# Loads, rounding and global rows of V for pairs 8 to 15, placed by tables at later quanta

## The chip, the cores and the metric

The kernel runs on one core of one Trainium2 chip. The metric is the device time of one execution in microseconds, as the median of several runs. The engines are named as in the profile: PE is TensorE's matrix multiplies, PEld its weight loads, DVE is VectorE, ACT is ScalarE, POOL is GpSimd and SP is SyncE, which here only issues DMA transfers. Each engine works through its own instructions strictly in the order in which they were recorded, and waits at the first one whose inputs or buffers are not ready.

## The reference: what is computed

An attention with a local band and a few global positions, followed by a two-layer block with a squared ReLU:

```
scores = (q @ k^T) / 8                       # 8 batches x 8 heads, 576 positions, 64 per head
mask   = |i - j| <= 32, or i or j is one of 8 global positions
attn   = softmax(where(mask, scores, -1e9))
x      = (attn @ v), heads side by side      # 4608 tokens x 512
out    = (s * relu(x @ w_in)**2 + b) @ w_out # 512 -> 2048 -> 512
```

Inputs and output are float32 in DRAM; the kernel multiplies in bfloat16.

## The kernel before

**Pairs.** Two heads make a pair: 32 pairs p, counted from 0 as in the code (the words "nine to sixteen" mean p = 8 to 15). Four pairs make a batch bi = p // 4. The 576 keys of a pair lie in 5 chunks of 120, in partitions 8 to 127 of a tile of 128 partitions (V), or 0 to 119 (K, Q); the 8 rows that are left hold the global keys.

**What a pair needs.** K and Q of a pair are loaded as float32 into staging (`natk`, `natq`, four slots each), rounded to bfloat16 on ACT (`round_k` L236 into `natb`, `round_q` L278), and transposed: K from pair 8 on by a DMA transpose on SP (`turn_k` L295, profile line L297), Q up to pair 17 by PE. DVE then writes the eight global columns into the transposed tile (`put_kq` L548, profile line L554), and only then PE may multiply with it. V is loaded into `natv` (`load_v`, L306, profile line L226; staging slot (p - 2) % 4), rounded into a ring `vring` of five slots (`cast_v` L309, profile line L312; ring slot p % 5), and its eight global rows are copied into the ring by a small DMA from `gvall` (`put_v` L541, profile line L543). For p of 16 and more, POOL's DMA loads V with the cast on the way, and nothing is rounded by an engine.

**Quanta.** The second half of the work (`moe_quanta` L741) is cut into quanta of four matmuls of 128x512. `run_pair` (L858) walks through eight steps s = 0 to 7 of a pair and issues one quantum in most of them, so that a place in the program is a pair (p, s): pair p, step s. Attention's work is hung on such places. `VISITS` (L47) says where PE visits a pair: at (8, 7), (9, 7), (10, 6), (11, 5) and then (12, 3), (13, 3) and so on. A visit to p multiplies Q and K of the second part of pair p and the first part of pair p + 1 (`visit` L849, tiles `pss` and `psw`), and then multiplies the probabilities of an earlier step with V (`put_out`, tile `po`): pairs 8 and 9 are first needed from `vring` at (9, 7), pairs 10 and 11 at (11, 5), pairs 12 and 13 at (13, 3), pairs 14 and 15 at (15, 3).

**What sets the order.** Everything is recorded by hand: `at(s, f, ...)` in the loop over p (L1120 to L1211) puts an operation behind the quanta of step s, `run_pair` puts others ahead of them. K and Q of later pairs, the K transposes, the V loads up to pair 15 and the global rows of pairs 8 to 15 all go out on SP, in one sequence. POOL rounds V of pairs 8 to 12, scatters global columns into the second block's input (L733), gathers and loads the pieces of w_out for the bias (`wpiece` L1099, profile line L1101). ACT rounds V of pairs 13 to 15.

**Where V of pairs 8 to 15 stands before.** Loads: pair 8 ahead of the steps of p = 4, pair 9 ahead of p = 5, pair 10 at (6, 5), 11 and 12 at (7, 5), 13 at (8, 5), 14 at (9, 5), 15 at (10, 5) (L1150 to L1154). Rounding: 8 and 9 at (7, 2), 10 at (8, 2), 11 at (9, 2), 12 at (10, 2) on POOL, 13 at (11, 2), 14 at (11, 4), 15 at (12, 4) on ACT (L888 to L900). Global rows: 8 and 9 at (7, 7), then pair p + 2 at (p, 7) (L1188 to L1191).

Of the kernel before, what the change touches and what calls it, by code (L numbers as in the profile page):

```python
# [34 lines left out]
NPAIR = B * H // 2  # L35
# [9 lines left out]
VCAST = 16  # L45
SOFT = 16
VISITS = {8 * p + {8: 7, 9: 7, 10: 6, 11: 5}.get(p, 3): p for p in range(JOIN, NPAIR)}  # L47
KT0 = 16
NX = 3
N6 = NCH * KC // NJ  # L50
# [25 lines left out]
def view(ap, *dims):  # L76

    return bass.AP(
        tensor=ap.tensor, offset=ap.offset, ap=[list(ap.ap[0])] + [list(d) for d in dims]
    )  # L80
# [3 lines left out]
def kernel(  # L84
# [12 lines left out]
    nc = tc.nc  # L97
# [33 lines left out]
    def bank(name):  # L131
# [4 lines left out]
        elif name in ("psh", "psg"):  # L136
            ago = min((when[0] - x for x in VISITS if x <= when[0]), default=8)
            left = min((x - when[0] for x in VISITS if x > when[0]), default=8)
            near = ago < 2 or left < 3 or ago == 4
# [64 lines left out]
    def v_slot(p):  # L204
        return p - 2 if p in (4, 5) else (p if p < 4 else p - 2) % NV
# [89 lines left out]
    def turn_k(p):  # L295
        kts[p] = kqp.tile([P, KT0 + NCH * P], BF16, tag="kt", name="kt")
        nc.sync.dma_start_transpose(  # L297
            out=kts[p][:, KT0:].rearrange("p (c x) -> p c x", x=P), in_=natb[:, p % NV]
        )
# [6 lines left out]
    def load_v(eng, p):  # L306
        load_nat(eng if p < VCAST else nc.gpsimd, "v", p)

    def cast_v(eng, p):  # L309
        if p >= VCAST:  # L310
            return
        eng(out=vring[:, p % NVR], in_=(natk if p in (4, 5) else natv)[:, v_slot(p)])  # L312
# [235 lines left out]
    def put_kq(p, which=(0, 1)):  # L548
        bb, x = divmod(p, 8)
        if p >= NSIX:  # L550
            ktile[p] = kts[p][:, KT0 - NG : KT0 - NG + LQ]
        for i in which:
            dst, src_ = ((ktile[p], gkt[bb]), (qbufs[p % 3][:, HB:], gqt[bb % 2]))[i]
            V(  # L554
                out=view(dst, [P, NCH], [1, NG]),
                in_=view(src_[:, NG * x : NG * x + NG], [0, NCH], [1, NG]),
            )
# [31 lines left out]
    def trans_a(p, later=later):  # L589
        ps = trans("k", p)  # L590
        kt = ktp.tile([P, LQ], BF16, tag="kt", name="kt")
        ktile[p] = kt[:]

        def evac():
            (A if p == 5 else V)(
                out=view(kt[:, NG:], [P, NCH], [NJ, KC // NJ], [1, NJ]),
                in_=view(ps, [KC // NJ, NCH], [1, KC // NJ], [NP6, NJ]),
            )
            if 3 < p < 6:
                put_kq(p)  # L600

        later.append(evac)
# [233 lines left out]
    def step():  # L836
        if pending:
            pending.pop(0)()

    def open_batch(bi):  # L840
        gsums[bi] = nrm.tile([P, 2, 2, 3, NG], FP32, tag="gs", name="gs")
# [5 lines left out]
    A, V, G = nc.scalar.copy, nc.vector.tensor_copy, nc.gpsimd.tensor_copy  # L847
# [10 lines left out]
    def run_pair(p, nq, extra):  # L858

        bi, hp = divmod(p, 4)  # L860
        if hp == 0 and p > 4:
            open_batch(bi)
        for s in range(8) if p > 4 else range(NCH, 8):
            prev, later[:] = list(later), []
            now = []
            at = 8 * p + s
            if p >= JOIN:
                when[0] = at
            if at in VISITS:
                visit(p)  # L870
            elif 4 < p < JOIN and s in ((0, 4) if p % 2 else (1, 3)) or (p, s) == (JOIN, 1):
                qk(p, int(s > 1))
            j = VISITS.get(at + 3, NPAIR) + 1
            if j < QTURN:
                trans_b(j, now)
            for x in (1, 2):
                if VISITS.get(at - x, 0) > JOIN:
                    step()
                    if x == 2 and VISITS[at - x] % 4 == 0:
                        later.append(lambda: scatter(bi - 1))  # L880
            if s < NCH:
                if s in (2, 3) and p <= JOIN:
                    step()
                if (p, s) == (JOIN, 4):
                    later.append(lambda: scatter(bi - 1))
                if s == 1 and p in (6, 7):
                    cast_v(A, p)
                if s == 2 and p == 7:  # L888
                    cast_v(G, 8)
                    cast_v(G, 9)  # L890
                if s == 2 and 7 < p < 11:
                    cast_v(G, p + 2)
                if p > 10:

                    eng, j = {
                        (3, 2): (A, p + 2), (3, 4): (A, p + 3), (0, 4): (A, p + 3),
                        (1, 2): (G, p + 3),
                    }.get((hp, s), (A, NPAIR))
                    if j < NPAIR:
                        cast_v(eng, j)  # L900
            elif s == 5:
                if 4 < p < JOIN - 1:
                    trans_b(p + 1, now)
            if (p, s) == (JOIN - 1, 6):
                trans_b(p + 1, now)
            if s == 4 and 4 < p < NSIX - 1:
                trans_a(p + 1, now)
            if s in (5, 6) and p < JOIN:
                step()
            for f in now + prev:  # L910
                f()
            if VISITS.get(at, 0) > JOIN or 4 < p <= JOIN and s == (4 if p % 2 else 1):
                put_out(p // 2 if p % 2 else p // 2 - 1, 1 - p % 2)
            if s == 3 and p in (6, 7):
                put_v(V, p)
            if s == 7 and p == 4:
                put_v(V, 4)
            if s == 2 and p == 5:
                cast_v(A, 5)
            if s == 3 and p == 5:  # L920
                put_v(V, 5)
            for f in extra.get(s, ()):
                f()
            Q(nq[s])
# [195 lines left out]
    for p in range(4, NPAIR):  # L1120
        bi, hp = divmod(p, 4)
        ex = {}

        def at(s, f, *a, ex=ex):
            ex.setdefault(s, []).append(lambda: f(*a))
# [10 lines left out]
        for s in range(8):  # L1136
            j = VISITS.get(8 * p + s + 2, NPAIR) + 1
# [4 lines left out]
        for j in range(p + 1, min(p + 7, NPAIR)):  # L1142
            x = {
                10: (6, 1), 11: (7, 4), 12: (7, 5), 17: (12, 0), 18: (13, 0), 19: (14, 0),
                20: (14, 4),
            }.get(j, (j - 5 if j < 17 else j - 6, 0))
            if j > 8 and x[0] == p:
                at(x[1], load_nat, nc.sync, "k", j) if x[1] else load_nat(nc.sync, "k", j)
                at(x[1], load_q, j) if x[1] else load_q(j)
        for j in {4: (8,), 5: (9,), 6: (10,), 7: (11, 12)}.get(p, (p + 5,)):  # L1150
            if p < 6:
                load_v(nc.sync, j)
            elif j < VCAST:
                at(5, load_v, nc.sync, j)  # L1154
        if p + 2 >= VCAST and p + 2 < NPAIR:
            at(1, load_v, nc.gpsimd, p + 2)
        if p == 5:
# [7 lines left out]
        for s in range(8):  # L1165
            for j in range(p + 1, min(p + 5, NPAIR)):
# [18 lines left out]
                    at(s, turn_k, j)  # L1185
                if j >= QTURN and (j - 3, 7) == (p, s):
                    at(s, turn_q, j)
        if p == 7:  # L1188
            at(7, put_v, None, 8)
        if p >= 7 and p + 2 < NPAIR:  # L1190
            at(7, put_v, None, p + 2)  # L1191
        if p == 6 or (p % 8 == 4 and 8 < p < NPAIR - 4):
            steps = globals_of((p + 5) // 8)
# [61 lines left out]
```

## Time and profile before

| | |
|---|---|
| median of 3 runs | 340.72 us (338.2, 340.72, 341.35) |
| the profiled execution | 338.03 us, its span 336.4 us |
| PE busy | 317.6 us, 94% of the span |
| PEld / DVE / ACT / POOL busy | 168.6 / 205.1 / 200.0 / 113.2 us |
| moved by DMA | 50.08 MB, of which SP's queue 28.33 MB and POOL's 20.77 MB |

The span is the time from the first to the last event on the core; the profiled execution's own time is 1.6 us more. A busy PE is not a PE at its peak, but idle time of PE is lost for good in a kernel whose PE is busy 94% of the time, unless what follows had to wait anyway. The other engines have slack on average; what counts of them is the one place at which PE waits for them.

### The profile page before, as it was taken

The numbers are of one execution on the slowest core, as the hardware profiler recorded it, in microseconds if no ns is written. First come the engines' busy times: TensorE is split into PE (matmuls) and PEld (weight loads), VectorE is DVE, ScalarE is ACT, GpSimd is POOL, SyncE is SP. The second block draws the span as 40 slices with busy tenths as digits, with TensorE's granted clock in tenths as the row PEclk, the third lists the DMA queues.
The fourth block names the chain that finished last, engine by engine and source line by source line (L and its number), as shares of the span: only waits on it lengthen the run. The fifth ranks groups of instructions, "written<-read, shape, count | busy, mean of one in ns | idle before, by whom it ended". The sixth has DMA issues, their size and how long they took to land.

```text
span 336.4 us, 8685 instructions
## 1 busy us (share of the span) xinstructions
PE 317.6 (94%) x3324; PEld 168.6 (50%) x3364; DVE 205.1 (61%) x540; ACT 200.0 (59%) x337; POOL 113.2 (34%) x220
## 2 busy tenths in 40 slices
PE   7688889799899999999999999999999999999995
PEld 4465344445454555467644444444467544444444
DVE  5479777566669588676765676567556524423422
ACT  3465778657895688557855885687268406404700
POOL 7841751225001405282368316822660030000000
PEclk9999999999999999999999999999999999999999
DMA  8999999997999999999999979993850010011011
GB/s 152 195 208 199 211 196 188 200 213 165 192 174 174 222 210 224 218 154 169 168 220 238 201 131 230 248 98 84 173 116 2 28 68 31 2 63 62 3 52 72
DMA packets 133533, 50.08 MB, mean 149 GB/s; under 512 B 122124, under 2 KB 128588, under 8 KB 133484
## 3 DMA queue, kind: packets, MB, share of 16 engines
q1 hardware_dynamic: 101346, 28.33, 51.3%
q0 software_dynamic: 31792, 20.77, 34.9%
q8 instruction: 26, 0.43, 0.6%
q10 hardware_dynamic: 354, 0.43, 0.4%
q14 instruction: 15, 0.12, 0.1%
HBM read 42.35 MB, written 9.44 MB: 154 GB/s over the span
## 4 chain that ended last, share of the span: by engine, by line
PE 70%; DMA 10%; issue 7%; POOL 5%; DVE 4%; ACT 3%; POOLq 1%; ACTq 0%; DVEq 0%
PE pso L789 31%; PE psh L756 30%; PE po L661 5%; DMA natq<-in_q_dram 4%; DMA kt<-natb 4%; DMA wst<-in_moe_w_out_dram 2%; PE pss L637 2%; ACT r L777 1%; PE psw L637 1%; DVE wsum L1105 1%; POOL xt L733 1%; POOL sixq L199 1%; POOL sixk L199 1%; POOLq L997 1%; DVE g L780 1%
## 5 line engine op out<-in xcount | busy, mean ns | idle before, releaser
L756 PE MATMUL psh<-xt,win_t 128*128 128x512 bf16 (+4 forms) x688 | 129.7, 340 | 2.4 <-POOL xt L733 0.9
L789 PE MATMUL pso<-wout_t,g 128*128 128x512 bf16 (+1 forms) x573 | 126.4, 373 | 2.4 <-issue 2.1
L777 ACT ACTIVATE r<-psh 128x512 bf16<-128x512 f32 x144 | 85.7, 599 | 58.2 <-PE psh L756 56.5
L756 PEld LDWEIGHTS <-win_t 128*128 128x128 bf16 x704 | 63.5, 98 | 58.7 <-issue 2.2
L789 PEld LDWEIGHTS <-g 128*128 128x128 bf16 x592 | 56.2, 98 | 62.9
L780 DVE TENSOR_TENSOR g<-r 128x512 bf16<-128x512 bf16 x144 | 60.3, 422 | 41.1 <-ACT r L777 40.2
L644 ACT ACTIVATE em<-pss 128x840 bf16<-128x840 f32 (+1 forms) x38 | 33.6, 884 | 43.5 <-PE pss L637 43.5
L645 DVE TENSOR_TENSOR em<-em,mask 128x904 bf16<-128x904 bf16 x64 | 38.6, 610 | 33.5 <-ACT em L644 31.2
L733 POOL COPY xt<-xg 128x4 bf16 (+1 forms) x72 | 17.4, 242 | 57.9 <-DVE xt L708 54.0
L809 DVE SCALAR_TENSOR_TENSOR osb<-pso,sb,bias_row 128x512 f32<-128x512 f32 (+1 forms) x25 | 18.2, 727 | 28.7 <-PE pso L789 28.4
L226 POOL DMA_DIRECT2D vring<-in_v_dram x33 | 29.4, 896 | 9.1 <-PE po L661 8.3
L708 DVE TENSOR_TENSOR xt<-po,rep 128x480 bf16<-128x480 f32 (+2 forms) x60 | 24.5, 449 | 3.5 <-ACT rep L718 2.6
L637 PEld LDWEIGHTS <-kt 64*128 64x128 bf16 x384 | 11.9, 99 | 20.2 <-issue 13.2
L644 ACT ACTIVATE em<-psw 128x904 bf16<-128x904 f32 x23 | 21.2, 924 | 0.1
L813 POOL DMA_DIRECT2D out_dram<-osb x16 | 9.1, 566 | 30.3 <-DVE osb L809 25.0
L661 PE MATMUL po<-em,vring 128*32 128x160 bf16 (+3 forms) x840 | 17.9, 220 | 0.7 <-DVE vring L543 0.5
L237 ACT CAST natb<-natk 128x640 bf16<-128x640 f32 x24 | 17.4, 727 | 1.8 <-DMA natk<-in_k_dram 1.8
L637 PE MATMUL pss<-qt,kt 64*128 64x192 bf16 (+4 forms) x228 | 14.6, 240 | 3.0 <-DVE qt L554 2.1
L715 ACT ACTIVATE ln<-po 128x324 f32<-128x324 f32 (+1 forms) x30 | 12.9, 429 | 5.7 <-PE po L661 5.7
L718 ACT ACTIVATE rep<-ln 128x324 f32<-128x324 f32 (+1 forms) x32 | 14.8, 461 | 0.3
L661 PEld LDWEIGHTS <-vring 128*32 128x32 bf16 x896 | 13.7, 98 | 1.1 <-issue 1.0
L661 PE MATMUL po<-em,onesb 128*32 128x192 bf16 (+2 forms) x360 | 11.5, 235 | 0.3 <-ACT rep L718 0.2
(126 smaller groups left out, 242.8 us busy)
## 6 DMA issues: line engine op xcount, KB each, us to landing
natk<-in_k_dram SPq DMA_DIRECT2D x47, 150.0 KB
natv<-in_v_dram SPq DMA_DIRECT2D x28, 150.0 KB
natq<-in_q_dram SPq DMA_DIRECT2D x55, 75.0 KB
wst<-in_moe_w_out_dram POOLq DMA_DIRECT2D x8, 512.0 KB, 6.5
out_dram<-osb POOLq DMA_DIRECT2D x16, 256.0 KB, 3.1
vring<-in_v_dram POOLq DMA_DIRECT2D x31, 75.0 KB, 5.3
out_dram<-osbh POOLq DMA_DIRECT2D x9, 256.0 KB, 3.8
win_t<-in_moe_w_in_dram POOLq DMA_DIRECT2D x4, 512.0 KB
```

What stands on the lines that cost most here:

```text
L226: eng.dma_start(out=dst[r : r + rows, n, c : c + nch, hh], in_=bass.AP(tensor=src[t].tensor, offset=o + c * KC * D, ap=[[D, rows], [KC * D ...
L637: nc.tensor.matmul(ps[:, hh, at : at + hi - lo], ktile[p][r, P * c : P * c + P], qbufs[p % 3][r, lo:hi], start=at == 0, stop=at + hi - lo ...
L644: nc.scalar.activation(em[:], ps[:, :, 0:n], AF.Exp, scale=SCALE)
L645: later.append(lambda: nc.vector.tensor_mul(em[:], em[:], masks[g]))
L661: nc.tensor.matmul(po[DH * j : DH * j + DH, a : a + n], view(vring[:, p % NVR, c, hh, part - 1 :], [2, DH]) if part else onesb[:], emt[(p, ...
L708: nc.vector.tensor_tensor(out=view(xt[:, 2 * g, x0 + t0 :], [NXT, 2], [w, runs], [1, w]), in0=view(po[:, STEP[blk] + col :], [STEP[blk], 2 ...
L733: nc.gpsimd.tensor_copy(out=xt[:, h, S * (bi % NX) : S * (bi % NX) + S][:, :, ds(greg_p[i], 1)], in_=xgs[bi][:, h, i : i + 1],)
L756: nc.tensor.matmul(psh[:, d0 : d0 + n], win_t[:, a, f * P : f * P + P], xt[:, a, x0 : x0 + n], start=(a == 0 and j == 0), stop=(a == 3), s ...
L777: nc.scalar.activation(r[:], psh, AF.Relu)
L780: later.append(lambda g=g, r=r: nc.vector.tensor_mul(g[:], r[:], r[:]))
L789: nc.tensor.matmul(pso[:, 0:nn], gl[f][:, u * P : u * P + P], wout_t[:, f, n0 : n0 + nn], start=(f == 0), stop=(f == 15),)
L809: nc.vector.scalar_tensor_tensor(out=osb[:, 0:nn], in0=pso[:, 0:nn], scalar=s_bc, in1=bias_row[:, n0 : n0 + nn], op0=OP.mult, op1=OP.add,)
```

## The change

Three tables take the place of the conditions that placed V of pairs 8 to 15. `VLOAD` gives the place of each load, `VROUND` the place and engine of each rounding (0 is ACT, 1 is POOL), `VGLOBAL` the place of each copy of global rows.

```
+VLOAD = {
+    8: (6, 6), 9: (7, 2), 10: (7, 6), 11: (8, 2), 12: (8, 6), 13: (9, 4), 14: (10, 4), 15: (11, 4),
+}
+VROUND = {
+    (7, 7): (1, 8), (8, 2): (1, 9), (8, 6): (1, 10), (9, 4): (1, 11), (10, 4): (1, 12),
+    (11, 2): (0, 13), (11, 4): (0, 14), (12, 4): (0, 15),
+}
+VGLOBAL = {
+    8: (8, 3), 9: (8, 4), 10: (8, 7), 11: (9, 6), 12: (10, 6), 13: (11, 7), 14: (12, 7), 15: (13, 7),
+}
...
-                if s == 2 and p == 7:
-                    cast_v(G, 8)
-                    cast_v(G, 9)
-                if s == 2 and 7 < p < 11:
-                    cast_v(G, p + 2)
...
+            if (p, s) in VROUND:
+                eng, j = VROUND[(p, s)]
+                cast_v((A, G)[eng], j)
...
-        for j in {4: (8,), 5: (9,), 6: (10,), 7: (11, 12)}.get(p, (p + 5,)):
-            if p < 6:
-                load_v(nc.sync, j)
-            elif j < VCAST:
-                at(5, load_v, nc.sync, j)
+        for j, x in VLOAD.items():
+            if x[0] == p:
+                at(x[1], load_v, nc.sync, j)
+        for j, x in VGLOBAL.items():
+            if x[0] == p:
+                at(x[1], put_v, None, j)
...
-        if p == 7:
-            at(7, put_v, None, 8)
-        if p >= 7 and p + 2 < NPAIR:
+        if VCAST <= p + 2 < NPAIR:
             at(7, put_v, None, p + 2)
```

No instruction is added or removed. The sequences of PE, DVE and ACT stay as they are, row for row. On POOL one of three roundings ahead of a scatter (that of pair 10) comes behind it. On SP the sequence changes in the stretch from Q of pair 9 to the transpose of K of pair 14. The order of SP's instructions shows it at three places. A row is a line of the kernel, the operation, what is written and read, its shape, and how many follow each other (two loads are one pair's K, V or Q).

First place, SP, before: behind Q of pair 9 come V of 8 and 9, K and Q of 10, V of 10, then the transposes of K 8 and K 9, then K of 11.

```order
L266 DMA natq<-in_q_dram 96x2x384
L226 DMA natv<-in_v_dram 120x5x64 x4
L226 DMA natk<-in_k_dram 120x5x64 x2
L266 DMA natq<-in_q_dram 96x2x384
L226 DMA natv<-in_v_dram 120x5x64 x2
L297 DMA_TRANSPOSE kt<-natb 128x5x128 x2
L226 DMA natk<-in_k_dram 120x5x64 x2
```

First place, SP, with the change (its lines are ten further down):

```order
L276 DMA natq<-in_q_dram 96x2x384
L236 DMA natk<-in_k_dram 120x5x64 x2
L276 DMA natq<-in_q_dram 96x2x384
L307 DMA_TRANSPOSE kt<-natb 128x5x128
L236 DMA natv<-in_v_dram 120x5x64 x4
L307 DMA_TRANSPOSE kt<-natb 128x5x128
L236 DMA natk<-in_k_dram 120x5x64 x2
```

Six V loads (pairs 8, 9 and 10) that stood ahead of the transpose of K 8 now stand behind it; those of pair 10 go still further down.

Second place, SP, before: V of 11 and 12, the transpose of K 10, the global rows of 8 and 9, K and Q of 13, V of 13, the transpose of K 11.

```order
L226 DMA natv<-in_v_dram 120x5x64 x4
L297 DMA_TRANSPOSE kt<-natb 128x5x128
L543 DMA vring<-gvall 8x5x128 x2
L226 DMA natk<-in_k_dram 120x5x64 x2
L226 DMA natq<-in_q_dram 120x5x64 x2
L226 DMA natv<-in_v_dram 120x5x64 x2
L297 DMA_TRANSPOSE kt<-natb 128x5x128
```

Second place, SP, with the change: V of 10, the transpose of K 10, K and Q of 13, V of 11, the global rows of 8 and 9, V of 12, the global rows of 10, the transpose of K 11.

```order
L236 DMA natv<-in_v_dram 120x5x64 x2
L307 DMA_TRANSPOSE kt<-natb 128x5x128
L236 DMA natk<-in_k_dram 120x5x64 x2
L236 DMA natq<-in_q_dram 120x5x64 x2
L236 DMA natv<-in_v_dram 120x5x64 x2
L553 DMA vring<-gvall 8x5x128 x2
L236 DMA natv<-in_v_dram 120x5x64 x2
L553 DMA vring<-gvall 8x5x128
L307 DMA_TRANSPOSE kt<-natb 128x5x128
```

The two copies of global rows no longer follow the transpose at once; six loads stand between.

Third place, SP, before: the transpose of K 11, the global rows of 10, K, Q and V of 14, the transpose of K 12, the global rows of 11, K, Q and V of 15, the transpose of K 13.

```order
L297 DMA_TRANSPOSE kt<-natb 128x5x128
L543 DMA vring<-gvall 8x5x128
L226 DMA natk<-in_k_dram 120x5x64 x2
L226 DMA natq<-in_q_dram 120x5x64 x2
L226 DMA natv<-in_v_dram 120x5x64 x2
L297 DMA_TRANSPOSE kt<-natb 128x5x128
L543 DMA vring<-gvall 8x5x128
L226 DMA natk<-in_k_dram 120x5x64 x2
L226 DMA natq<-in_q_dram 120x5x64 x2
L226 DMA natv<-in_v_dram 120x5x64 x2
L297 DMA_TRANSPOSE kt<-natb 128x5x128
```

Third place, SP, with the change: the transpose of K 11, K and Q of 14, V of 13, the global rows of 11, the transpose of K 12, K and Q of 15, V of 14, the global rows of 12, the transpose of K 13.

```order
L307 DMA_TRANSPOSE kt<-natb 128x5x128
L236 DMA natk<-in_k_dram 120x5x64 x2
L236 DMA natq<-in_q_dram 120x5x64 x2
L236 DMA natv<-in_v_dram 120x5x64 x2
L553 DMA vring<-gvall 8x5x128
L307 DMA_TRANSPOSE kt<-natb 128x5x128
L236 DMA natk<-in_k_dram 120x5x64 x2
L236 DMA natq<-in_q_dram 120x5x64 x2
L236 DMA natv<-in_v_dram 120x5x64 x2
L553 DMA vring<-gvall 8x5x128
L307 DMA_TRANSPOSE kt<-natb 128x5x128
```

V of pair 14, which stood ahead of the transpose of K 12, now stands where V of pair 15 stood, ahead of the transpose of K 13. The place at which ACT rounds pair 14 in its own sequence has not moved.

## Rows read from the trace of the kernel before

**Rows 1.** The page: busy time of the engines, and DMA's busy share in 40 slices.

```profile
PE 317.6 (94%) x3324; PEld 168.6 (50%) x3364; DVE 205.1 (61%) x540; ACT 200.0 (59%) x337; POOL 113.2 (34%) x220
DMA  8999999997999999999999979993850010011011
```

**Rows 2.** Windows: stretch, length, busy time of each engine, clock, DMA share, GB/s.

```profile
40.00:60.00 20.00, 18.78 (x230) 8.90 (x232) 14.83 (x39) 16.20 (x29) 7.58 (x12) 1.00 1.19 194
60.00:80.00 20.00, 17.91 (x182) 8.99 (x176) 11.76 (x30) 10.65 (x18) 8.35 (x16) 1.00 0.93 186
80.00:100.00 20.00, 18.70 (x233) 9.58 (x235) 13.00 (x34) 18.54 (x34) 1.13 (x2) 1.00 1.25 197
100.00:120.00 20.00, 19.68 (x215) 9.96 (x219) 14.94 (x43) 12.85 (x23) 4.88 (x12) 1.00 1.20 193
```

**Rows 3.** Timeline of PE: start, length, instructions, and [idle before, ended by].

```profile
66.50 0.37 PE L637 MATMUL pss<-qt,kt 64*128 64x160 bf16 x6 [1.82 <-DVE qt L554]
...
81.47 0.58 PE L661 MATMUL po<-em,vring 128*32 128x160 bf16 x28
...
89.79 0.37 PE L637 MATMUL psw<-qt,kt 64*128 64x160 bf16 x6 [1.04 <-DVE kt L554]
...
103.26 0.36 PE L637 MATMUL psw<-qt,kt 64*128 64x160 bf16 x6
```

**Rows 4.** Chain of work that ended last: start, length, the transfer waited for.

```profile
61.72 4.24 DMA kt<-natb
...
81.27 8.27 DMA kt<-natb
```

**Rows 5.** Timeline of SP: start and length of issuing, transfers.

```profile
53.29 5.61 SPq L226 DMA_DIRECT2D natv<-in_v_dram  x4
...
60.68 0.94 SPq L226 DMA_DIRECT2D natv<-in_v_dram  x2
61.72 3.35 SPq L297 DMA_TRANSPOSE kt<-natb  x2
...
73.62 1.21 SPq L297 DMA_TRANSPOSE kt<-natb  x1
75.20 1.62 SPq L543 DMA_DIRECT2D vring<-gvall  x2
76.87 1.29 SPq L226 DMA_DIRECT2D natk<-in_k_dram  x2
...
95.43 1.43 SPq L226 DMA_DIRECT2D natv<-in_v_dram  x2
97.03 1.62 SPq L297 DMA_TRANSPOSE kt<-natb  x1
```

**Rows 6.** Timeline of ACT, two roundings: of K 10, and of V 14.

```profile
63.41 0.72 ACT L237 CAST natb<-natk 128x640 bf16<-128x640 f32 x1 [1.47 <-DMA natk<-in_k_dram]
...
95.79 0.72 ACT L312 CAST vring<-natv 128x640 bf16<-128x640 f32 x1
```

**Rows 7.** Timeline of DVE ahead of the put of K 8, and at K 13.

```profile
63.71 0.22 DVE L685 TENSOR_REDUCE gs<-po 128x24 f32<-128x72 f32 x1
64.55 0.85 DVE L708 TENSOR_TENSOR xt<-po,rep 128x120 bf16<-128x120 f32 x2 [0.62 <-ACT rep L718]
66.05 0.32 DVE L554 COPY kt<-gkt 128x40 bf16<-128x40 bf16 x1 [0.66 <-DMA kt<-natb]
...
100.58 0.47 DVE L611 COPY qt<-pst 128x600 bf16<-128x600 bf16 x1 [0.38 <-PE pst L569]
...
102.68 0.18 DVE L554 COPY kt<-gkt 128x40 bf16<-128x40 bf16 x1 [0.66 <-DMA kt<-natb]
```

**Rows 8.** Windows of 2 us, columns as in Rows 2.

```profile
76.00:78.00 2.00, 2.00 (x14) 0.95 (x12) 0.89 (x2) 0.60 (x1) 1.85 (x3) 1.00 0.09 17
78.00:80.00 2.00, 2.00 (x15) 0.97 (x13) 1.69 (x5) 1.44 (x3) 1.70 (x3) 1.00 0.68 159
```

**Rows 9.** Timeline of POOL: the first pieces of w_out; landing of gvall's transfers.

```profile
79.56 1.57 POOL L1101 DMA_DIRECT2D wst<-in_moe_w_out_dram  x2
...
DMA to landing us min/median/max: 3.7/5.0/6.4
```

More of the change, by code (lines that the diff above doesn't have):

```diff
@@ L887, in run_pair @@
                     cast_v(A, p)
-                if s == 2 and p == 7:
-                    cast_v(G, 8)
-                    cast_v(G, 9)
-                if s == 2 and 7 < p < 11:
-                    cast_v(G, p + 2)
[L893 to L900, printed above, removed]
             elif s == 5:
```

## The prediction

> **What bounds the kernel now.** I read the page first: PE is busy 317.6 of 336.4 us [rows 1], so only some 19 us of PE's idle time are there to win anywhere, and DMA is nearly full for the first two thirds. Then the windows: from 40 to 100 us PE idles 1.22 + 2.09 + 1.30 = 4.6 us, against 0.32 in the 20 us behind [rows 2]. The change touches nothing ahead of 40 us, so about 4.6 - 3 x 0.32 = 3.6 us is the most that it can give. Third, PE's timeline names two gaps in that stretch: 1.82 us ahead of 66.50, at (8, 1), and 1.04 us ahead of 89.79, at (10, 6) [rows 3]. Both are ended by DVE's put into a transposed K, and the chain of waits names what the put waited for: the transposes of K 8 (issued at 61.72, 4.24 us) and of K 11 (81.27, 8.27 us) [rows 4]. Last, SP's timeline: it issues without a real pause through this stretch, and six V loads that took 5.61 and 0.94 us stand ahead of K 8's transpose [rows 5]. So until about 100 us the kernel is bound by SP's queue and the DMA engines behind it. Whatever the change wins for K is paid by what now stands later in the same queue, and the question is who waits for that.
>
> **Gap one, K 8, at (8, 1).** PE was free at 66.50 - 1.82 = 64.68 [rows 3]. Without 5.61 + 0.94 us of V loads ahead [rows 5], the transpose can be issued near 61.72 - 6.55 = 55.2 and lands by 59.5, at the 4.24 us of [rows 4]. The put then no longer waits for DMA; next late is DVE itself. Ahead of the put it scales a result that waits for ACT, which sat 1.47 us idle for K 10 [rows 6]; K 10 is also loaded earlier now, so that wait goes, and the scaling starts behind the reduction, at 63.71 + 0.22 = 63.93, takes 0.85, and the put 0.32 [rows 7]: 65.1. PE starts at 65.2 in place of 66.50: **gain 1.3 us**. Bounds: nothing, if DVE is held by something else, and the whole 1.82.
>
> **Gap two, K 11, at (10, 6).** Ahead of its transpose stand one V load less and one small copy more, and POOL's first pieces of w_out, issued at 79.56 [rows 9] and in flight beside that transpose before, now wait for the rounding of V 12 and come after it. I take the 4.24 us of the quieter transpose: 81.27 + 4.24 = 85.5 or earlier, against PE's need at 89.79 - 1.04 - 1.3 = 87.5. **Gain 1.04 us**; at the noisy 8.27 us it would be 89.5, and gap one's gain would be lost again here. The first end is nearer, since the w_out pieces are what fell away.
>
> **The puts of global rows 8 and 9, needed at (9, 7).** They move behind K 13, Q 13 and V 11, a net of two loads, about 1 us of issuing. Before they were issued from 75.20 to 76.8 [rows 5], and PE's V multiplication at 81.47 did not wait [rows 3]. It now comes at 81.47 - 1.3 = 80.2, the puts at about 77.8. POOL's transfers of the same source landed in 3.7 to 6.4 us [rows 9], which gives 81.5 to 84.2: a wait of 0 to 4 us. I take nothing, since before only 4.7 us lay between issue and use and nothing waited, and since the queue ahead of them starts earlier. A short wait here is not added to what follows; it would only let ACT come later to the next place.
>
> **V 14, rounded by ACT at (11, 4).** This is where the change pays. ACT's sequence is unchanged: it came to that rounding at 95.79 [rows 6] and comes 2.34 us (1.3 + 1.04) earlier, at 93.45. V 14 now stands in SP's queue where V 15 stood, and that was issued at 95.43 [rows 5]. The transpose directly behind it was issued at 97.03 [rows 5] and DVE could use it at 102.68, having waited for it [rows 7]: 5.6 us. With the same 5.6 us V 15 landed at about 101.0. Ahead of V 14 there is one V load less, 1.43 us: 99.6. And there is a hole to be filled: DMA was busy only 0.09 and 0.68 of 76 to 80 us [rows 8], (0.91 + 0.32) x 2 = 2.46 us lost, because between 73.62 and 76.87 SP issued only a transpose and two small copies [rows 5]. With six loads between the transpose and those copies, the engines have work then. So V 14 lands between 97.1 (hole filled) and 99.6 (not filled). I take **97.1**, because the loads that fill it are a matter of order alone.
>
> Behind that rounding ACT has the next K to round and the exponentials of the visit at (11, 5); DVE waits for these and stands ahead of its own put of K 13, without which PE can't start the visit at (12, 3). Before, from the rounding's start to the end of that put it was 102.86 - 95.79 = 7.07 us, of which 0.66 was a wait for the transpose and 0.38 one for PE [rows 7], both over earlier now: 6.03 us. So the put ends at 97.1 + 6.03 = 103.1 and PE starts at 103.2, where it started at 103.26 before [rows 3] and would be ready at 100.9. The 2.34 us won are given back.
>
> **Behind that.** PE had no wait for K or V after 100 us (0.32 us idle in 20 us [rows 2]); V 15 lands some 6 us behind V 14, near 103, and ACT comes to it only after the exponentials of (12, 3), at about 105. From the transpose of K 14 on SP's sequence is the old one. POOL's wait ahead of its roundings costs nothing: it idles.
>
> **The sum.** 1.3 + 1.04 - 2.3 = 0.0 us: 338.0 against the profiled execution's 338.03. Its time lies 2.7 us under the median of the runs; the four executions shown (338.03, 338.2, 340.72, 341.35) have a mean of 339.6, and I put the forecast there: **339.6 us, no change**.
>
> **Rivals.** *A: loads land soon after they are issued, and V 14 is in time.* By the order above SP issues V 14 near 95.43 - 1.43 - 2.46 = 91.5 to 93. For it: SP is ready early. Against: the 8.27 and 4.24 us of [rows 4]. If V 14 lands by 93.45, all 2.34 us stay: 335.7 on the profiled level, 337.3 on the mean; with gap one wholly gone 0.5 less. The Trainium skill, page "DMA: Bandwidth & Descriptors", section "Anatomy of one DMA", gives a transfer some 2.0 us fixed plus its bytes at 436 GB/s, a fit for transfers issued from GpSimd: 2.35 us for 150 KB, an estimate by which V 14 lands at 95.3 and 1.9 of the 2.34 us stay. The trace disagrees as long as the queue is full: 4.24 and 8.27 us [rows 4].
>
> *B: slower.* The hole is not filled, since SP again runs into its limit of transfers in flight, and V 14 lands at 99.6. Place: ACT at (11, 4). The put of K 13 ends at 105.6, PE starts 105.7: 2.4 us later than before, 340.4 on the profiled level, 342.0 on the mean. It decides from a landing at 97.2 on, and each us later costs one us. For it: DMA moved 193 to 197 GB/s behind 80 us at a share above 1 [rows 2], so the backlog there is one of bytes, and the w_out pieces, now later, fall on V 13 and V 14. Against: they fell ahead of V 15 before, too.
>
> *C: the loads weren't what held K 8.* Then gap one stays, ACT comes to V 14 1.3 us later, and the time is the same as forecast; only the trace would tell.
>
> **Numbers.** Forecast 0.58, C within it; A 0.22; B 0.20. What a measurement of this kernel can tell from no change is 1%, 3.4 us. The forecast's own range is that of the runs, 338.2 to 341.4. A reaches 337.3 on the mean and 1.5 less in a run like the lowest; B reaches 342.0 and 1.2 more in one like the higher: 335.8 to 343.2. Faster by over 1% (under 337.3): two thirds of A, 0.15, and 0.04 of the forecast: 0.19. Slower by over 1% (over 344.1): half of B, where V 14 lands later still, 0.10, and 0.04: 0.14. The rest, 0.67, is within 1%.
>
> **What would show it.** Right: no wait of PE for a put of K at (8, 1) beyond 0.5 us, none at (10, 6); ACT idle 3 to 4 us ahead of a rounding L322, ended by DMA natv; and PE waiting 2 to 3 us at (12, 3) for the put of K 13. Wrong: ACT doesn't idle for natv (A), or idles 6 us (B); DMA's share from 76 to 80 us stays low; PE waits at (9, 7) for global rows. What would upset the sum is any wait of PE behind 105 us, where I count none.

## The result, and the profile after

The changed kernel takes **343.46 us** in the median of 4 runs (342.99 to 346.75) beside 339.68 of 4 runs of the kernel before (338.20 to 341.35): ratio 1.0138, 95% interval 1.0091 to 1.0185. It is slower, by 3.8 us or 1.1% in the medians and 1.4% in the ratio; I had forecast no change, 339.6 us with a range up to 343.2. A second measurement gave 1.0122 (1.0044 to 1.0199), again 3.8 us in the medians. Here and below medians are those of all runs, while ratios leave out runs over 1.5% above the fastest of the same kernel, so a ratio is not the quotient of the medians.

The profiled execution took 343.84 us, its span is 342.2. The first rows that answer to [rows 2] are the windows of 20 us (stretch, length, busy time of PE, PEld, DVE, ACT, POOL, clock, DMA share, GB/s):

```profile
40.00:60.00 20.00, 18.87 (x218) 8.82 (x221) 15.34 (x40) 17.14 (x31) 8.60 (x14) 1.00 1.21 208
60.00:80.00 20.00, 19.74 (x207) 9.87 (x210) 12.10 (x33) 11.63 (x20) 4.45 (x11) 1.00 1.17 177
80.00:100.00 20.00, 18.27 (x225) 9.19 (x223) 11.14 (x29) 13.32 (x24) 5.79 (x6) 1.00 1.09 185
100.00:120.00 20.00, 16.01 (x165) 7.78 (x167) 11.54 (x31) 11.70 (x19) 4.89 (x12) 0.83 1.08 161
```

From 60 to 80 us PE now idles 0.26 us in place of 2.09: what the change was to win there is won. From 100 to 120 it idles 4.0 us in place of 0.3, and the granted clock there is 0.83 where it was 1.00. PE's timeline names the places (start, length, instructions, and in brackets the idle time ahead and what ended it), to be held against [rows 3]:

```profile
65.40 0.37 PE L647 MATMUL pss<-qt,kt 64*128 64x160 bf16 x6
...
81.37 0.81 PE L671 MATMUL po<-em,vring 128*32 128x160 bf16 x28 [0.82 <-DMA vring<-gvall]
...
88.72 0.36 PE L647 MATMUL psw<-qt,kt 64*128 64x160 bf16 x6
...
103.68 0.66 PE L579 MATMUL pst<-ident,sixq 120*128 120x120 bf16 x5 [4.32 <-ACT em L654]
104.13 5.05 PE L799 MATMUL pso<-wout_t,g 128*128 128x512 bf16 x12
109.12 0.35 PE L647 MATMUL pss<-qt,kt 64*128 64x92 bf16 x6
```

Both gaps ahead of a put of K are gone, at (8, 1) and at (10, 6). There is a wait of 0.82 us for the global rows of pairs 8 and 9 at (9, 7), and one of 4.32 us at (12, 0), where PE transposes the next Q. Behind it 12 matmuls of w_out take 5.05 us; in the profile of before the same 12 took 2.76 us:

```profile
100.38 2.76 PE L789 MATMUL pso<-wout_t,g 128*128 128x512 bf16 x12
```

The windows of 2 us of the profile after (columns as above) show why:

```profile
100.00:102.00 2.00, 0.00 (x0) 0.00 (x0) 0.00 (x0) 0.49 (x1) 0.00 (x0) 0.99 1.15 113
102.00:104.00 2.00, 0.32 (x4) 0.32 (x4) 0.34 (x1) 2.00 (x4) 0.00 (x0) 0.50 1.14 167
104.00:106.00 2.00, 2.00 (x9) 0.87 (x7) 1.78 (x4) 2.00 (x5) 0.00 (x0) 0.50 1.38 167
106.00:108.00 2.00, 2.00 (x7) 0.61 (x5) 1.79 (x7) 1.00 (x2) 0.00 (x0) 0.50 1.26 185
```

While PE stands idle the granted clock falls from 1.00 (2.4 GHz) to 0.50 (1.2 GHz), and it stays there through the matmuls behind the wait. The Trainium skill, page "TensorE: Matmul & The Clock Gate", section "Part 1: The HAM clock gate", says so too: the clock is at half rate in an idle engine, and activity releases it; the rows agree.

Who held PE? The transposition writes into a bank that the exponentials of (11, 5) must have read. ACT's timeline, against [rows 6]:

```profile
94.22 0.67 ACT L787 ACTIVATE r<-psh 128x512 bf16<-128x512 f32 x1
101.51 0.72 ACT L322 CAST vring<-natv 128x640 bf16<-128x640 f32 x1 [6.62 <-DMA natv<-in_v_dram]
102.14 0.72 ACT L247 CAST natb<-natk 128x640 bf16<-128x640 f32 x1
102.77 0.86 ACT L654 ACTIVATE em<-pss 128x840 bf16<-128x840 f32 x1
```

ACT came to the rounding of V14 at 94.9 us, and V14 landed at 101.4: the exponentials, ready to run, stand behind it. And SP's timeline (start, length of issuing) of the loads of K15, Q15 and V14, against [rows 5], then the chain of waits, and the first w_out pieces on POOL behind its roundings of V11 and V12:

```profile
88.03 1.28 SPq L236 DMA_DIRECT2D natk<-in_k_dram  x2
89.36 5.17 SPq L236 DMA_DIRECT2D natq<-in_q_dram  x2
94.57 1.68 SPq L236 DMA_DIRECT2D natv<-in_v_dram  x2
```

```profile
76.67 4.66 DMA vring<-gvall
...
95.39 6.02 DMA natv<-in_v_dram
```

```profile
81.20 2.22 POOL L322 CAST vring<-natv 128x640 bf16<-128x640 f32 x2 [5.82 <-ACT em L654]
...
85.94 1.57 POOL L1101 DMA_DIRECT2D wst<-in_moe_w_out_dram  x2
```

SP issued the load of Q15 for 5.17 us, then V14, whose second transfer took 6.02 us. The w_out pieces left POOL at 85.94 in place of 79.56 [rows 9], just ahead of that. In the kernel before SP issued K15 later, but Q15 in 1.05 us:

```profile
93.29 1.00 SPq L226 DMA_DIRECT2D natk<-in_k_dram  x2
94.34 1.05 SPq L226 DMA_DIRECT2D natq<-in_q_dram  x2
```

The hole in DMA's work from 76 to 80 us [rows 8] is filled:

```profile
76.00:78.00 2.00, 2.00 (x16) 1.04 (x14) 1.22 (x4) 1.20 (x2) 0.00 (x0) 1.00 1.30 180
78.00:80.00 2.00, 2.00 (x19) 0.90 (x18) 1.10 (x5) 1.92 (x4) 0.00 (x0) 1.00 1.00 154
```

Place by place, from the starts of PE's visits in the two profiles (us, after less before):

| stretch | before | after | difference | forecast |
|---|---|---|---|---|
| start to (7, 0) | 56.39 | 57.33 | +0.94 | 0 |
| (7, 0) to (8, 1): gap one | 10.11 | 8.07 | -2.04 | -1.3 |
| (8, 1) to (9, 7) | 14.28 | 14.29 | 0 | 0 |
| (9, 7) to (10, 6): global rows | 7.62 | 8.84 | +1.22 | 0 |
| (10, 6) to (11, 5): gap two | 7.92 | 6.70 | -1.22 | -1.04 |
| (11, 5) to (12, 3): V14 | 6.75 | 13.89 | +7.14 | +2.34 |
| (12, 3) to the end | 233.3 | 233.1 | -0.2 | 0 |

The first row lies ahead of the change but for its last 3 us or so. The sum is 5.8 us, the difference of the spans; the medians differ by 3.8, and below it shows that the profile of before is of an early execution.

### The profile page after: what moved, and what is told of

Read it like the earlier page. It is cut to its first block, busy times and chain, and to the rows that moved or that the text cites. A ratio compares the mean times of both kernels' runs of the same rounds, so it can differ in the third digit from the quotient of the medians.

```text
span 342.2 us, 8682 instructions
## 1 busy us (share of the span) xinstructions
PE 319.8 (93%) x3324; PEld 169.0 (49%) x3364; DVE 205.1 (60%) x540; ACT 199.9 (58%) x337; POOL 114.0 (33%) x220
## 4 chain that ended last, share of the span: by engine, by line
PE 73%; issue 7%; SPq 6%; POOL 3%; DMA 3%; DVE 3%; ACT 3%; POOLq 1%; ACTq 0%
PE pso L799 32%; PE psh L766 31%; PE po L671 5%; SPq L236 4%; PE pss L647 2%; DMA natv<-in_v_dram 2%; SPq L307 1%; DMA vring<-gvall 1%; PE psw L647 1%; POOL xt L743 1%; PE psf L957 1%; POOLq L997 1%; ACT r L787 1%; POOL gf L404 1%; ACT em L654 1%
## 5 line engine op out<-in xcount | busy, mean ns | idle before, releaser
L799 PE MATMUL pso<-wout_t,g 128*128 128x512 bf16 (+1 forms) x573 | 128.7, 378 | 2.4 <-issue 2.1
```

The lines of the kernel that those rows point to most:

```text
L799: nc.tensor.matmul(pso[:, 0:nn], gl[f][:, u * P : u * P + P], wout_t[:, f, n0 : n0 + nn], start=(f == 0), stop=(f == 15),)
```

## The experiments

The first theory: ACT's wait for V14 makes PE's at (12, 0), and this the half clock, 4.3 + 2.4 us. Its rival: SP's queue is late as a whole, and without V14 something else in it would hold PE. All kernels are the changed one with the edit shown, unless it says otherwise. Times are medians; ratios are to the kernel before, run on the same chip. "From (7, 0)" means by PE's timeline in that run's profile.

**V14 rounded by POOL.**

```
-(11, 4): (0, 14),
+(11, 7): (1, 14),
```

> V14 is rounded by GpSimd at (11,7) in place of ScalarE at (11,4); its load and everything else stay as in the change. Theory: ScalarE's 6.6 us wait for V14 holds the exponentials of (11,5), these hold TensorE 4.3 us at the transposition of Q at (12,0), and the halved clock behind it costs 2.4 us more; so the wait and the half clock go, GpSimd waits in ScalarE's place with nothing due behind it before 114 us, and the time is 343.5 - 6.7 = about 337, 0.99 of before. Rival: SyncE's queue as a whole is late, and TensorE finds the next late thing (the turned K13 or K14) in the place of V14: 340 to 343. The granted clock between 102 and 110 us tells them apart too: 1.00 by the theory.

Measured: 341.36 us (11 runs), ratio 1.0009 (0.9966 to 1.0053). The profile is of the slowest of these runs, 347.87 us, which came to (7, 0) only at 65.3 us. The wait at (12, 0) and the half clock there are gone in it; the visit at (12, 3) comes 43.5 us behind (7, 0) in place of 51.8. But ACT's next rounding met the same fate, for V15:

```profile
115.26 0.72 ACT L322 CAST vring<-natv 128x640 bf16<-128x640 f32 x1 [4.08 <-DMA natv<-in_v_dram]
```

PE waited 2.65 us for it at pair 13, at half clock behind. The loss against before is taken away, but not 6.7 us; that something else in the queue is late, as the rival says, this one profile can only suggest.

**V14 loaded earlier on SP.**

```
-14: (10, 4),
+14: (9, 5),
```

> V14 is loaded at (9,5), ahead of the turning of K12 on SyncE's queue, in place of (10,4); ScalarE still rounds it at (11,4). Theory: V14 lands at about 90 us, before ScalarE asks for it at 94.9, and the 4.3 us wait at (12,0) and the half clock go; but the two loads (about 1.7 us of the queue) now lie ahead of the turning of K12, which has no slack at (11,5), so TensorE waits 1 to 2 us there: 338 to 339. Rival A (it is not V14's landing): 343.5 as the change. Rival B (K12 is late by more): the gain is all given back at (11,5), 341 or over.

Measured: 340.90 us (10 runs), ratio 1.0016 (0.9966 to 1.0065). ACT's row for V14 has no wait, and the price is where the theory put it, at (11, 5), only smaller:

```profile
98.46 0.71 ACT L322 CAST vring<-natv 128x640 bf16<-128x640 f32 x1
```

```profile
99.16 0.37 PE L647 MATMUL psw<-qt,kt 64*128 64x160 bf16 x6 [0.56 <-DVE kt L564]
...
102.78 0.43 PE L579 MATMUL pst<-ident,sixq 120*128 120x120 bf16 x5
```

The median is over the 338 to 339 that I gave. Two ways of taking V14 out of ACT's way, with SP's order unchanged in one and ACT's in the other, both end level with before. That V14 at (11, 4) makes the loss is shown; that the time does not fall below before is not yet explained.

**Zeros in the wait.** The edit, shortened (place 96 is (12, 0)):

```
+if at == 96:
+    for _ in range(18): matmul(open output bank, zeros, zeros)
 if j < QTURN:
     trans_b(j, now)
```

> 18 matmuls of zeros, added into the output bank that is open, run on TensorE ahead of the transposition of Q at (12,0), in the time in which TensorE waited there 4.3 us (18 by 0.22 us = 4.0 us); the result is unchanged. Theory: the wait for ScalarE stays and ends at the same time, but the granted clock stays at 1.00 and the 12 matmuls behind it take 2.7 us in place of 5.05: 343.5 - 2.4 = about 341. Rival (the clock falls for another reason than the idle time): the 12 matmuls still take 5 us, 343.5 or a little over.

Measured: 342.99 us (10 runs), ratio 1.0068 (1.0023 to 1.0114). V14 lands at 101.2, as in the changed kernel (101.4), PE is not idle ahead of (12, 0), the clock is 1.00 in every window of 2 us from 92 to 108, and:

```profile
100.64 4.05 PE L888 MATMUL pso<-dummy 128*128 128x512 bf16 x18
104.52 0.43 PE L579 MATMUL pst<-ident,sixq 120*128 120x120 bf16 x5
104.79 2.76 PE L800 MATMUL pso<-wout_t,g 128*128 128x512 bf16 x12
```

The same 12 matmuls take 2.76 us: the idle time is the cause of the half clock, 5.05 - 2.76 = 2.3 us. The times don't show it clearly: this kernel stands 2.8 us above before in the medians, the changed one 3.8, and the intervals of the ratios overlap (the profile has a new wait of 2.15 us for K12 at (11, 5)).

**The w_out pieces later.**

```
-for s in {12: (2, 3, 4), ...
+for s in {12: (), ...
...
-if p in (11, 12, 14, 15):
+if p in (12, 14, 15, 16):
```

> The eight pieces of w_out that GpSimd loads for the bias are loaded one or two pairs later (at (12,6), (14,6), (15,6), (16,6)), so that the first two leave GpSimd at about 116 us in place of 86. Theory: these pieces (0.5 MB each) are what slowed the turning of K12, the load of Q15 and V14 behind them; without them V14 lands at about 97 to 98 us, as I had forecast, ScalarE's wait shrinks from 6.6 to about 2.5 us, TensorE's at (12,0) from 4.3 to under 0.5, no half clock: 337 to 338.5. Rival: SyncE's own queue is what is full, V14 lands at 100 or later without the pieces, 342 to 343.5.

Measured: 345.12 us (4 runs), ratio 1.0136 (1.0025 to 1.0248): no gain. The profile splits that in two. In the stretch asked about, SP issues Q15 in 1.05 us in place of 5.17 and V14 at 92.67 in place of 94.57:

```profile
91.57 1.05 SPq L236 DMA_DIRECT2D natq<-in_q_dram  x2
```

```profile
98.76 0.72 ACT L322 CAST vring<-natv 128x640 bf16<-128x640 f32 x1 [3.57 <-DMA natv<-in_v_dram]
```

```profile
100.92 0.42 PE L579 MATMUL pst<-ident,sixq 120*128 120x120 bf16 x5 [1.36 <-ACT em L654]
101.18 2.76 PE L799 MATMUL pso<-wout_t,g 128*128 128x512 bf16 x12
...
154.81 4.45 PE L766 MATMUL psh<-xt,win_t 128*128 128x192 bf16 x24 [4.21 <-DVE osbh L816]
```

V14 lands at 98.7, PE waits 1.36 us, the clock stays at 1.00 and (12, 3) is reached 47.5 us behind (7, 0), in place of 51.8. More than all of it is lost at 150.6: DVE's sum of the pieces now waits 6.98 us for a piece, and PE waits 4.21 us behind DVE. So the pieces are part of V14's lateness: in the four profiles that start within 1 us of this one with the pieces at 86, V14 is rounded 43.4 to 44.7 us behind (7, 0), here 42.4, 1.0 to 2.3 us sooner. In those four SP issued Q15 for 2.93 to 5.17 us. Summed over the trace's DMA packets from 90 to 94.5 us, POOL's queue moved 126 GB/s and SP's 53 in the changed kernel; here POOL's moved nothing and SP's 201. The Trainium skill, page "DMA: Bandwidth & Descriptors", section "Queues, rings and completion order", says that each DMA engine takes turns, packet by packet, between the queues that have work for it; this run agrees in direction.

**V14 and V15 by POOL.**

```
-(11, 4): (0, 14), (12, 4): (0, 15),
+(11, 7): (1, 14), (12, 4): (1, 15),
```

> V14 and V15 are both rounded by GpSimd (at (11,7) and (12,4)), none by ScalarE behind V13. In the run with V14 alone on GpSimd, ScalarE waited 4.1 us for V15 in the place of V14, and TensorE 2.6 us at pair 13. Theory: with both gone from ScalarE no wait of TensorE between (11,5) and pair 13 is left, the granted clock stays at 1.00 there, and from (7,0) to the end it takes 284.9 - 6.7 = about 278 us (before: 280.0); the median is 337 to 339. Rival: the queue is late as a whole and the turned K (K13, K14) is next: 280 or over, 340 to 342.

Measured: 340.36 us (10 runs), ratio 1.0049 (1.0002 to 1.0095). No wait of PE between (8, 1) and pair 13, (12, 3) 43.5 us behind (7, 0), and 279.0 us from (7, 0) to the end beside 280.0 in the profile of before, with two new waits, 0.5 and 1.3 us, behind (12, 3). The mechanism came as expected, the gain in the medians did not.

**Global rows of 8 and 9 ahead of V11.**

```
 VLOAD                VGLOBAL
-11: (8, 2), ...      8: (8, 3), 9: (8, 4), ...
+11: (8, 5), ...      8: (8, 2), 9: (8, 3), ...
```

> The global rows of pairs 8 and 9 are put on SyncE's queue ahead of the loads of V11 in place of behind them (V11's load 8 to 9 instructions later); V14 stays on ScalarE. Theory: the puts land some 1.7 us sooner (two loads of 0.85 us less ahead of them), so the wait of 0.8 us at (9,7) goes; V11, 1.6 us later, holds only GpSimd. V14 lands as late as in the change, so nearly all that is won is lost again at (12,0), where TensorE waits for ScalarE at an absolute time: median within 1 us of the change, 342.5 to 344. Rival (the puts wait for what the rounding of V9 or GpSimd does, not for the queue): the wait at (9,7) stays at 0.8 us.

Measured: 344.70 us (4 runs), ratio 1.0185 (1.0036 to 1.0334). No wait at (9, 7); but PE came to (7, 0) 4 us later in this execution, so the profile alone does not show that the order did it. At (12, 0) the loss stands:

```profile
105.62 0.42 PE L579 MATMUL pst<-ident,sixq 120*128 120x120 bf16 x5 [3.23 <-ACT em L654]
105.88 4.44 PE L799 MATMUL pso<-wout_t,g 128*128 128x512 bf16 x12
```

**Gap one alone.** V8 to V10 as in the change; V11 to V15 loaded ahead, rounded and put as before.

```
 VLOAD = { ...
-11: (8, 2), 12: (8, 6), 13: (9, 4), 14: (10, 4), 15: (11, 4),
+11: (7, 6), 12: (7, 7), 13: (8, 5), 14: (9, 5), 15: (10, 5),
```

> One part of the change alone: V8, V9, V10 are loaded, rounded and put as in the change; V11 to V15 are loaded one step behind V10 or where the kernel before has them (V14 at (9,5), V15 at (10,5)), and rounded and put as there. Theory: gap one (1.8 us at (8,1)) goes as in the change; V14 is early, so no wait at (12,0) and no half clock; the puts of 8 and 9 come behind two more loads, so the wait at (9,7) is 1 to 3 us; gap two stays, about 1 us. From (7,0) to the end 279 to 281 us against 280.0, median 338.5 to 341. Rival (the loss of the change comes from V8 to V10 too): 342 or over.

Measured: 340.56 us (10 runs), ratio 1.0072 (1.0030 to 1.0114). The wait for the global rows is just over what I expected, and costs a half clock that I had not counted:

```profile
83.36 0.81 PE L671 MATMUL po<-em,vring 128*32 128x160 bf16 x28 [3.12 <-DMA vring<-gvall]
84.10 5.31 PE L766 MATMUL psh<-xt,win_t 128*128 128x512 bf16 x16
```

16 such matmuls take 3.63 us at the full clock. With two more loads ahead of those two small copies the wait at (9, 7) is 3.12 us, beside 0.82 and 0 in two profiles of the changed kernel. Gap two, which I expected to stay, isn't there, since PE comes later to it by then; from (7, 0) to the end it takes 282.8 us, over the 279 to 281 that I gave.

**Three edits together:** V14 and V15 by POOL, puts of 8 and 9 ahead of V11, and the first two w_out pieces ahead of V11's rounding on POOL (`p in (9, 12, 14, 15)`, at step 3 for pair 9).

> Three edits together: V14 and V15 rounded by GpSimd, the puts of pairs 8 and 9 ahead of V11's load, and the first two pieces of w_out issued ahead of V11's rounding on GpSimd (about 75 us in place of 86). Theory: the waits at (9,7), (11,5) and (12,0) all go or stay under 0.5 us, the clock stays at 1.00, and both gaps stay closed: from (7,0) to the end 284.9 - 6.7 - 0.8 = about 277, median 336 to 338, under before by 0.5 to 1.0%. Rival: the pieces, earlier, slow the turning of K11 or K13 and the puts at 76 to 82 us instead, and a wait of 1 to 3 us appears at (9,7) or (10,6): 338 to 341.

Measured: 340.35 us (10 runs), ratio 1.0041 (1.0001 to 1.0081). The one wait of PE from 62 us to the end that is over 0.2 us is 0.45 us, at (9, 7); (7, 0) to the end is 277.6 us. By the two first profiles this should have beaten both kernels, and it came out level with before: what I held it against was in doubt, not its own rows.

**PE made late on purpose.** 18 zero matmuls, 4.06 us, ahead of (7, 2), in the kernel before and in the changed one.

```
+if at == 57:
+    for _ in range(18): matmul(spare bank, zeros, zeros)
```

(Shortened; place 57 is (7, 1), and the matmuls stand in the timeline behind the visit at (7, 0).)

> The kernel before, with 18 matmuls of zeros (4.0 us, into a bank that nobody reads) on TensorE ahead of (7,2), behind the visit at (7,0): from there on TensorE is 4 us late, and SyncE's queue is not held by it directly. Theory (the late rows of K8 and K11 land at times that the queue sets, not TensorE): the gaps of 1.8 us at (8,1) and 1.0 us at (10,6) are both absorbed, so the time grows by about 1.1 us only: 340.5 to 341.5 in the median against 339.5. Rival (the queue follows TensorE's pace): both gaps stay, +4 us, 343.5.

> The changed kernel with the same 4.0 us of zero matmuls ahead of (7,2). Theory (V14's landing at 101 us is set by the queue, not by TensorE): the wait at (12,0) shrinks from 4.3 to about 1 us, the wait at (9,7) goes, and the clock does not fall, so useless work of 4 us makes the kernel no slower: 343.5 + 4.0 - 0.8 - 3.2 - 2.4 = about 341, under the change itself. Rival (V14's load follows TensorE's pace through the engines that free its buffers): the waits stay as they are, 347.

Measured: the kernel before with zeros 342.40 us (10 runs), ratio 1.0096 (1.0055 to 1.0137), 3.5 us above the median of before. The changed kernel with zeros 343.23 us (4 runs), ratio 1.0147 (1.0078 to 1.0215), beside 342.68 without: useless work of 4.06 us costs 0.6 us in the medians, which rest on 4 runs each, some 4 us apart. Its rows at (12, 0):

```profile
102.69 0.42 PE L579 MATMUL pst<-ident,sixq 120*128 120x120 bf16 x5 [2.28 <-ACT em L654]
102.95 2.76 PE L799 MATMUL pso<-wout_t,g 128*128 128x512 bf16 x12
```

V14 landed at 100.5 (100.3 in the changed kernel on the same chip), so SP's queue did not follow PE's 4 us: it is 0.2 us later, 1.3 if counted from (7, 0). The theory holds here, with a wait of 2.28 where I expected 1; the median is 2 us over what I gave. In the kernel before both gaps are gone in the profile, but that execution was also 3 us late at (7, 0), and the median rose by nearly the rival's 4 us. That would fit if the gaps were small in most executions without zeros, too.

**The changed kernel again.**

> The changed kernel once more, unaltered, for a second profile: the first had ScalarE waiting 6.6 us for V14 and TensorE 4.3 us at (12,0). A load of V in the first 30 us lands up to 9 us late in some profiles of this study, in all kernels. Theory: where that wait is short, V14's wait at (12,0) is 3 to 4.5 us again; where it is long, TensorE comes later and the wait at (12,0) is shorter by as much. Rival: the 6.6 us were a single bad landing; 0 to 1 us here at the same start. Median 343 to 344.5.

Measured: 342.68 us (4 runs), ratio 1.0122 (1.0044 to 1.0199). ACT waits 6.65 us for V14, PE 4.44 us at (12, 0), and the clock is 0.50 from 102 to 106: the first profile was no accident. Not every run is like it: the fastest of the four, 341.25 us, had a mean clock of 1.00, so no half clock of this length.

**The start.** The three edits together, and the first of the four loads of w_out behind the first scatter.

> The three edits together as before (V14 and V15 on GpSimd, puts of 8 and 9 ahead of V11, first pieces of w_out for the bias early) and, in the start, the first of the four loads of w_out behind the first scatter (about 32 us) in place of 22 us. Theory: the load of V3, which VectorE waits for by 0 to 9 us at about 28 us, collides there with GpSimd's queue as V14 does at 94; with 0.5 MB less ahead of it the wait falls to 0 to 3 us and the runs lie closer together: median 336.5 to 338.5. Rival (V3 collides with w_in, or its lateness has another cause): the waits stay, 339.5 to 340.5; or the later piece slows V6 to K8 behind 34 us, 340 or over.

Measured: 343.57 us (4 runs), ratio 1.0175 (1.0095 to 1.0255). The wait for V3 is gone in this profile and (7, 0) comes at 55.83, but the second rival fits: the time is over 340, and the global rows are late at (9, 7), twice, with the half clock behind them.

```profile
83.16 0.25 PE L671 MATMUL po<-em,vring 128*32 128x160 bf16 x2 [1.76 <-DMA vring<-gvall]
85.13 0.94 PE L671 MATMUL po<-em,vring 128*32 128x160 bf16 x26 [1.73 <-DMA vring<-gvall]
86.00 5.92 PE L766 MATMUL psh<-xt,win_t 128*128 128x512 bf16 x16
```

**The kernel before, three more profiles,** unaltered. The new theory: the gaps that I priced belong to executions that start early.

> The kernel before, unaltered, for a profile of another execution. The place (7,0) was reached at 56.4 us in the profile that the prediction rests on, and between 55.8 and 65.3 us in the others of this study. Theory: the gaps at (8,1) and (10,6), 1.8 and 1.0 us, shrink by about as much as (7,0) is later than 56.4 us, and are gone from 60 us on, so that closing them is worth nothing in such an execution. Rival: SyncE's queue starts later by as much, and both gaps are as large at any start.

> The kernel before once more, as in the run ahead: by the theory the sum of the two gaps is 2.9 us where (7,0) is reached at 56.4, about 1 us at 58.4 and 0 from 60 us on; by the rival it is 2.9 us at any start.

> The kernel before a third time, as in the two runs ahead, for a further start: the sum of the gaps 2.9 us at 56.4, 1 at 58.4, 0 from 60 us on by the theory; 2.9 us by the rival.

Measured: 340.48, 341.38 and 339.73 us, one execution each, all on one chip. The first one's timeline of PE, with the row that makes it late and the visits at (7, 0), (8, 1), (10, 6) and (12, 3):

```profile
47.34 0.94 PE L661 MATMUL po<-em,vring 128*32 128x160 bf16 x26 [4.61 <-DVE vring L543]
...
62.23 0.37 PE L637 MATMUL pss<-qt,kt 64*128 64x160 bf16 x6
...
70.30 0.37 PE L637 MATMUL pss<-qt,kt 64*128 64x160 bf16 x6
...
92.39 0.36 PE L637 MATMUL psw<-qt,kt 64*128 64x160 bf16 x6
...
105.73 0.36 PE L637 MATMUL pss<-qt,kt 64*128 64x92 bf16 x6
```

No brackets at the visits: neither gap is there. Its SP issues the transposes of K8 (with K9) and of K11 here:

```profile
62.24 4.53 SPq L297 DMA_TRANSPOSE kt<-natb  x2
...
82.18 1.22 SPq L297 DMA_TRANSPOSE kt<-natb  x1
```

In the first profile these stood at 61.72 and 81.27 [rows 5], in the three late ones at 61.59 to 62.66 and at 81.92 to 83.31: SP is at most 2.0 us later where PE is 4.5 to 5.9 us later. So the rival is out. The profiles side by side (us):

| profile | (7, 0) | gaps one and two | (7, 0) to (12, 3) | (7, 0) to the end |
|---|---|---|---|---|
| before, first | 56.39 | 1.82 + 1.04 | 46.68 | 280.0 |
| before, again | 60.89 | 0 + 0 | 43.76 | 277.2 |
| before, again | 62.23 | 0 + 0 | 43.50 | 276.6 |
| before, again | 62.29 | 0 + 0 | 43.51 | 277.5 |
| changed, first | 57.33 | 0 + 0 | 51.79 | 284.9 |
| changed, again | 56.92 | 0 + 0 | 51.13 | 284.3 |
| V14 and V15 by POOL | 59.25 | 0 + 0 | 43.50 | 279.0 |
| three edits | 61.81 | 0 + 0 | 44.23 | 277.6 |

The theory holds from 60.9 us on; between 56.4 and 60.9 there is no profile of the unaltered kernel before.

Four profiles don't say how often an execution is early. Of runs without a profile the mean granted clock is on record: it was 0.999 in the early profile of before and 0.990 to 0.994 in the three late ones, whose wait of 4.1 to 4.6 us at 47 us has a half clock behind it. Of the 63 other runs of the kernel before that were measured beside the experiments, 17 had 0.998 or more (2 of 25, 9 of 25 and 6 of 13 on three chips). By this sign, which is no proof, about one execution in four starts early and has the gaps.

## Why the prediction was wrong

- **Gap one**, "gain 1.3 us" (bounds 0 to 1.82): the gap of 1.82 went wholly, 2.04 with what lay around it. **Gap two**, "gain 1.04 us": 1.22. Against the one profile that I had, both are right in mechanism and a little small. Against the medians they were worth little: in three of four profiles of the kernel before the gaps don't exist, because PE comes later and finds K8 and K11 landed, and by the clock most other runs are like these three. My sum was made against an execution that I knew to lie 2.7 us under the median, and I carried its difference over unchanged. An early start is fast *and* has gaps; it was the same fact twice.
- **The puts at (9, 7)**, "a wait of 0 to 4 us. I take nothing": 0.82 us of wait, 1.22 with the rest; 0 in the second profile. My own figures there, a landing at 81.5 to 84.2 against a need at 80.2, gave 1.3 to 4 and not 0; taking nothing was a guess that came out near. As I said there, a wait here only let ACT come later.
- **V14 at (11, 4)** is the step that failed. The mechanism came as forecast (ACT idle for natv), but V14 landed at 101.4 us, behind both ends of "between 97.1 (hole filled) and 99.6 (not filled)". The hole at 76 to 80 us was filled (DMA share 1.30 and 1.00 in place of 0.09 and 0.68), and as far as K15 the time was won: SP issued it at 88.03 in place of 93.29. I took that for time won at V14. Then the issue of Q15 took 5.17 us in place of 1.05, so V14 was issued at 94.57, only about 0.9 us earlier than V15 stood there [rows 5], and it landed 6.8 us later, where I had counted 5.6. Of the 4.3 us behind my 97.1, 0.9 is the later start of this execution. One part, 1.0 to 2.3 us, is the w_out pieces, which I had moved out of gap two's way in the text and then not charged to V14. I named them in rival B, and set them aside because "they fell ahead of V 15 before, too": there they left POOL at 79.56, some 16 us ahead of V15's issue, here 8.6 us ahead of V14's. The rest I can't assign.
- **Where PE meets it.** I followed ACT's delay to the put of K13 and PE's visit at (12, 3). PE stops earlier, at (12, 0): the Q transposition needs the bank that the exponentials read. I had only followed data, not the banks that a late reader keeps.
- **The clock** was in no term. An idle time of 4.32 us was followed by 12 matmuls at half the clock, 2.3 us more; the zeros took just that away.
- **Rival B** came nearest: ACT idle for 6 us, and of its reasons the w_out pieces fall on V14. Its ground, a hole that is not filled, did not come, and it was mis-sized: its price stood at a landing of 99.6. "It decides from a landing at 97.2 on, and each us later costs one us": 4.2 us later cost 4.3, and the clock came on top.
- **Behind (12, 3)**, "where I count none": right in this profile, 233.1 us beside 233.3.

What stays open: why V14 takes 6 us from its issue, beyond the w_out pieces; and why the two best versions stand 0.4 to 0.5% above before (their intervals begin at 1.0001 and 1.0002), where their time from (7, 0) on is within 2.4 us of before's. A hint, no more: the six runs with V14 and V15 by POOL whose mean clock is 0.998 or more have a mean of 340.0 us, the nine such runs of before on the same chip 338.0. No version beat the kernel before.

## What to carry to other kernels

A gap in one profile is a race between two streams: before pricing it, ask how far each stream's arrival wanders from one execution to the next, and take a second profile if the profiled time is not the median. When a load is moved later, look for the in-order engine that touches it first: rounding on ACT put a transfer's landing ahead of exponentials that were ready, and an engine with nothing due behind it (POOL) took the same wait for nothing. And price a wait of PE of some us as the wait and the slow matmuls behind it.

## What the runs showed of the hardware

The granted clock fell to half behind single idle times of PE of 4.32, 4.44, 3.23, 3.12 and 2.65 us, and cost 2.3 us over 12 matmuls behind the first, and 1.7 each over 12 (4.44 beside 2.76) and over 16 (5.31 beside 3.63) behind the waits of 3.23 and 3.12; behind 2.28, 2.15 and 1.36 us it stayed at 1.00. The length of a wait alone does not sort these runs: behind one of 1.94 us, at 45.45 in the profile with V14 and V15 by POOL, it fell too. Two waits of 1.76 and 1.73 us with 0.25 us of work between them also ended in 16 slow matmuls (5.92 us). Zeros kept the clock as well as real data did.

While POOL's w_out pieces were moved, SP's queue got less and SP was slow to issue: 53 GB/s beside POOL's 126 and 4.51 us for the second load of Q15, where without the pieces it was 201 GB/s and 0.50 us.
